# The memory rows as the moving operand: check and V projection turned round, and an If around the fallback loop

## The chip, the core and the metric

The kernel runs on one core of one Trainium2 chip. The time is device microseconds from start to end of one execution. Before the change the median of 6 runs is 1271.91 us (lowest 1271.03, highest 1274.84).

## The reference

Two independent parts are computed and their results are laid side by side in the last axis. Part A is a diagonal state-space layer (`h = Lam_bar * h + Bu` over 2048 steps, then a product with C). Part B is attention with a recurrent memory, and the change lies in it:

```python
for s in range(n_seg):                       # 64 segments of 32 rows
    h = jnp.concatenate([mem, xs], axis=1)   # 8 memory rows + 32 rows of x
    q, k, v = (jnp.einsum('btd,dhe->bhte', h, W) for W in (Wq, Wk, Wv))
    scores = jnp.einsum('bhqe,bhke->bhqk', q, k) * scale
    p = _softmax(jnp.where(mask, scores, -1e9), axis=-1)
    o = jnp.einsum('bhqk,bhke->bhqe', p, v)
    o = jnp.einsum('bhte,hed->btd', o, Wo)
    mem = o[:, :M, :].copy()                 # the next segment's memory
    outs.append(o[:, M:, :])
```

There are 32 heads of 128, the model width is 1024, and everything large is bf16. The memory of a segment is the output of the segment before, so the loop is serial as written.

## The kernel before

The kernel does not walk through the segments one after the other. It guesses the memory of every segment, computes all segments at once from the guess, and afterwards compares the memory that comes out with the guess. If they differ by more than a tolerance, a loop over the 64 segments (`general`, L795 on) computes part B again in the serial way; with the inputs given here the comparison holds and the loop runs no time.

Four stages follow each other, all bound to the same TensorE:

- **Stage 1** (0 to about 364 us): part A's scan, and V of all rows of x for the eight groups of four heads (`v_x`). V rows go to DRAM tensors `b_vx` and `b_vt`.
- **Stage 2** (to about 487 us): part A's product with C, 32 half tiles of 32 matmuls of 512 columns. Between them the guess is made (`guess`, L495): for each of eight chunks of 128 of the model width, 32 matmuls (one for each head) with a chunk of Wo as the stationary operand and 64 columns of `b_ogT` as the moving one, into one PSUM tile. Its result has the model width on partitions. DVE writes it to the memory columns of `b_xe` (`memT`, 73 columns: one for each memory row that is distinct) and once more to `b_gx`, in the order of the comparison. Eight PE transposes turn `b_gx` into rows, and DVE copies these to `b_gm` [73, 1024].
- **Attention** (to about 1047 us): Q and K projections (`proj`) and attention (`attention`) are generators whose steps are interleaved. A unit of attention is 4 score matmuls into `psS` (L607), Exp on ACT (L610), a mask product on POOL into one of five `b_m` tiles (L613), and for three blocks at a time a matmul with V into `psO` or `psR`, with a reciprocal and a product on DVE (L629, L630). The product of the masked scores is used by TensorE one to two units later.
- **Output projection** (to the end): 16 tiles of 128 rows in two halves, each 32 matmuls of 512 columns, evicted by DVE and ACT in turn and stored. After the tiles of block 1 `check` (L749) is run.

`v_mem` (L521) computes V of the 73 memory rows for one group of four heads: 8 matmuls with `memT` (128x73) stationary and 512 columns of `b_wv` moving, giving [73, 512] in a `psP` tile; DVE casts it into `b_vst` (L89), and SP issues two DMAs, to `b_vx` and `b_vt`. It is called twice in stage 2, and six times in the attention stage, every second head pair at the unit u = 4.

`check` takes `b_omT` (the attention outputs of the 73 memory rows, transposed) as the stationary operand and 512 columns of Wo as the moving one: 32 matmuls for each half. DVE subtracts `b_gm`, ACT squares the output and the difference, with a sum along each row (L767, L768). Some one-column operations of DVE make `c_bad` of it, a matmul with ones (`psR<-c_bad,ones`) gathers the partitions, and `b_flag` is 0 or 1. At the end every engine reads the flag into a register, multiplies it by 64 and enters the loop with that count (L1078).

`psP` has three buffers that rotate over all users; `psS` two, `psO` two, `psR` one. In stage 1 the order on PE and SP is that of the program. Later on, a scheduler puts the instructions of each engine in order and can move independent ones past each other. Every engine executes its own queue in that order. Nearly all matmuls and copies go through helpers, so their lines are L62 (PE and SP), L87 (ACT) and L89 (DVE), and the tiles' names tell them apart (`t` and `wo` are the two halves of Wo, `a_hl` and `t` in stage 2 are part A's operands).

Of the kernel before, what the change touches and what calls it, by code (L numbers as in the profile page):

```python
# [25 lines left out]
H = 32; E = 128; SEG = 32; M = 8; NSEG = 64; L = M + SEG  # L26
# [9 lines left out]
NM = NTL + NMX  # L36
# [296 lines left out]
class PartB:  # L333
    def __init__(self, k, x, mem0, Wq, Wk, Wv, Wo, out):
        self.k = k
        self.x, self.mem0, self.out = x, mem0, out
        self.Wf = [w.rearrange("(c p) h e -> p c (h e)", p=128) for w in (Wq, Wk, Wv)]
        self.Wo = Wo.rearrange("h e d -> e h d")
        self.vx = [k.drp.tile([NSLOT, 4 * EV], BF16, name=f"b_vx{i}") for i in range(HB)]
        self.vt = [k.drp.tile([NTL, 4 * EV], BF16, name=f"b_vt{i}") for i in range(HB)]  # L340
        self.on = [k.drp.tile([T, 1024], BF16, name=f"b_on{i}") for i in range(4)]
        self.tn = [k.drp.tile([NR, 1024], BF16, name=f"b_tn{i}") for i in range(4)]
        c = k.cst
        self.m0T = c.tile([128, KC, M], BF16, name="b_m0T")
        self.omT = c.tile([128, H, NR], BF16, name="b_omT")
        self.gm = c.tile([NM, D], BF16, name="b_gm")
# [148 lines left out]
    def guess(self, pool):  # L495
        k = self.k; V, PE = k.V, k.PE
        pg = k.ps("S")
        for q in range(4):
            wo = self.wog.pop(0)
            for dc in range(2):  # L500
                c = 2 * q + dc
                for h in range(H):
                    PE.matmul(pg[:, c * NSEG:(c + 1) * NSEG], wo[:, h, dc * 128:(dc + 1) * 128], self.ogT[:, h, :], start=(h == 0), stop=(h == H - 1))
                yield
        pv = pg[:].rearrange("p (c s) -> p c s", c=KC)
        m = self.memT
        V.tensor_copy(m[:, :, NMX + 1:NMX + 2], pv[:, :, 0:1])
        V.tensor_copy(m[:, :, NMX + 3:NM], pv[:, :, 1:NSEG])

        gx = pool.tile([128, KC, NM], BF16, name="b_gx", bufs=1)  # L510
        V.tensor_copy(gx[:, :, 0:2], pv[:, :, 0:2])
        V.tensor_copy(gx[:, :, 2:NTL - 1], pv[:, :, 1:NSEG])
        V.tensor_copy(gx[:, :, NTL - 1:NM], pv[:, :, 0:1].to_broadcast([128, KC, NMX + 1]))
        pt = k.ps("R", (128, 1024), BF16)
        for c in range(KC):
            PE.transpose(pt[0:NM, c * 128:(c + 1) * 128], gx[:, c, :], k.ident[:])
        V.tensor_copy(self.gm[:], pt[0:NM, :])
        yield


    def v_mem(self, hb, w=None):  # L521
        k = self.k
        w = w or self.load_wv(hb)
        p = k.ps("P")
        for c in range(KC):
            k.PE.matmul(p[0:NM, :], self.memT[:, c, :], w[:, c, :], start=(c == 0), stop=(c == KC - 1))
        st = self.next_st()
        k.copy("v", st[0:NM, 0, :, 0:E], p[0:NM, :].rearrange("p (h e) -> p h e", h=4))
        sv = st[:, 0, :, :].rearrange("p h e -> p (h e)")
        k.SP.dma_start(self.vx[hb][64:64 + NMX, :], sv[0:NMX, :])  # L530
        k.SP.dma_start(self.vt[hb][:], sv[NMX:NM, :])
# [217 lines left out]
    def check(self):  # L749
        k = self.k; V, S, PE = k.V, k.S, k.PE  # L750
        pool = self.p4

        def small(name, n):
            return pool.tile([128, n], FP32, name=name, bufs=1)
        for q in range(4):
            k.SP.dma_start_transpose(self.omT[:, 8 * q:8 * q + 8, :], self.tn[q][:])
        dn = small("c_dn", 4)
        V.memset(dn[:], 0.0)
        for half in range(2):
            hs = slice(half * 512, (half + 1) * 512)  # L760
            p = k.ps("P")
            for h in range(H):
                PE.matmul(p[0:NM, :], self.omT[:, h, 0:NM], self.wo[half][:, h, :], start=(h == 0), stop=(h == H - 1))
            df = pool.tile([NM, 512], FP32, name="c_df", bufs=1)
            jk = pool.tile([NM, 512], FP32, name="c_jk", bufs=1)
# [16 lines left out]
        V.tensor_scalar(bad[:], ok[:], -1.0, 1.0, ALU.mult, ALU.add)  # L782
        pf = k.ps("R")
        PE.matmul(pf[0:1, 0:3], k.ones[:], bad[:], start=True, stop=True)
        fl = small("c_fl", 1)
        V.tensor_reduce(fl[0:1, :], pf[0:1, 0:3], AX.X, ALU.max)
        V.tensor_scalar(fl[0:1, :], fl[0:1, :], 0.5, None, ALU.is_ge)
        V.tensor_copy(self.flag[:], fl[0:1, :])
        if getattr(k, "dbg", None) is not None:
            k.SP.dma_start(k.dbg[:, 0:4], dn[:])  # L790
            k.SP.dma_start(k.dbg[:, 4:7], ok[:])
        yield

# [117 lines left out]
def kernel_main(tc, A_x, A_Lre, A_Lim, A_Bre, A_Bim, A_Cre, A_Cim, A_logdt, A_Dskip, B_x, B_mem0, B_Wq, B_Wk, B_Wv, B_Wo, out,  # L911
                force=False, dbg=None):
    with ExitStack() as ctx:
        k = K(tc, ctx)
# [15 lines left out]
        with pool("p1x", "right") as p1x, pool("p1", "right", 1) as p1:  # L930
# [28 lines left out]
            for kind, pc, q in order[1:]:  # L959
# [9 lines left out]
                n = 4 * pc + q  # L969
# [173 lines left out]
```

## Time and profile before

| what | value |
|---|---|
| median of 6 runs | 1271.91 us (1271.03 to 1274.84) |
| the profiled execution | 1275.58 us |
| its span, first to last instruction | 1273.9 us |
| its mean granted TensorE clock | 0.994 |
| PE busy | 1252.8 us (98%), 7860 matmuls |
| DVE, POOL, ACT busy | 52%, 22%, 21% |
| last matmul, last ACT copy | about 1267.4 us; 1268.14 us |

A line of the timeline gives the start, the duration, engine, source line, operation, output and inputs, shapes and the number of instructions merged in it; a note in brackets is the idle time of the engine before it and what ended that. For matmuls, `128*73 128x512` is the stationary operand's size (partitions x columns) and then the moving operand's. Matmuls are pipelined: a row of several lasts until the last one has left the array, which is later than when the next row starts. The time that a matmul costs the stream is thus the distance between the starts of two rows, divided by the count, and not the mean duration.

### The profile page before, as it was taken

Reading aid. Unit: us, or ns where it says so; the run is one execution under the profiler, and the core shown is the slowest. Engines: PE = TensorE matmul, PEld = TensorE weight load, DVE = VectorE, ACT = ScalarE, POOL = GpSimd, SP = SyncE. Lnnn points to the kernel's source line nnn. Section 1 sums busy time; section 2 is a strip of 40 time slices with the busy share of each in tenths; the row PEclk is TensorE's granted clock in tenths of the full one; section 3 lists DMA queues with packets and bytes.
Section 4 is the critical chain, followed back from the end, with each engine's and each line's share of the span. In section 5 each row is a group of like instructions: output and inputs, shape, how many; then the busy total and the mean of one; then the engine's idle time right before and its main releaser. Section 6 shows DMA issues by size and latency. Waiting matters only on the chain. (4 is left out here: it accounts for less than half of the span.)

```text
span 1273.9 us, 19279 instructions
## 1 busy us (share of the span) xinstructions
PE 1252.8 (98%) x7860; PEld 655.8 (51%) x7860; DVE 665.7 (52%) x1235; ACT 263.3 (21%) x632; POOL 277.3 (22%) x407
## 2 busy tenths in 40 slices
PE   8899999999999999999999999999999999999997
PEld 4344444444445545565556555555655554444443
DVE  3687899998711123666666666656666641001000
ACT  4244334443310000121212111212211110001000
POOL 3111322222322220322322232223222220000000
PEclk9899999999999999999999999999999999999999
DMA  9965436544799629245464544636474389215000
GB/s 201 238 194 165 136 113 148 141 125 133 193 357 305 204 77 237 69 93 133 104 144 104 138 104 109 138 75 137 95 158 92 66 221 224 69 37 129 17 25 19
DMA packets 317156, 174.12 MB, mean 137 GB/s; under 512 B 140808, under 2 KB 302848, under 8 KB 317064
## 3 DMA queue, kind: packets, MB, share of 16 engines
q1 hardware_dynamic: 294504, 147.53, 48.3%
q10 hardware_dynamic: 21536, 22.16, 5.5%
q0 software_dynamic: 1024, 3.17, 0.8%
q8 instruction: 63, 1.03, 0.4%
q14 instruction: 29, 0.24, 0.1%
HBM read 86.42 MB, written 52.19 MB: 109 GB/s over the span
## 5 line engine op out<-in xcount | busy, mean ns | idle before, releaser
L62 PE MATMUL psP<-b_wv,b_xe 128*128 128x512 bf16 (+2 forms) x1112 | 243.1, 376 | 4.9 <-ACT b_vst L87 3.6
L62 PE MATMUL psP<-b_xe,b_wq 128*128 128x480 bf16 (+1 forms) x1280 | 247.8, 343 | 0.0
L62 PE MATMUL psP<-b_xe,b_wk 128*128 128x480 bf16 (+1 forms) x1280 | 247.7, 343 | 0.0
L613 POOL TENSOR_TENSOR b_m<-b_e,maskB 99x396 bf16<-99x396 bf16 x160 | 139.4, 871 | 338.8 <-ACT b_e L610 338.8
L610 ACT ACTIVATE b_e<-psS 99x396 bf16<-99x396 f32 x176 | 88.2, 501 | 545.1 <-PE psS L62 542.3
L62 PEld LDWEIGHTS <-b_xe 128*128 128x128 bf16 (+1 forms) x1112 | 109.6, 99 | 130.8 <-issue 6.0
L62 PEld LDWEIGHTS <-b_wk 128*128 128x128 bf16 x1280 | 119.7, 98 | 95.8
L62 PEld LDWEIGHTS <-b_wq 128*128 128x128 bf16 x1280 | 118.5, 98 | 88.2 <-issue 0.2
L89 DVE CAST b_k<-psP 128x480 bf16<-128x480 f32 (+1 forms) x192 | 98.0, 532 | 98.1 <-PE psP L62 98.1
L89 DVE CAST b_q<-psP 128x480 bf16<-128x480 f32 (+1 forms) x192 | 98.2, 533 | 93.4 <-PE psP L62 91.6
L62 PEld LDWEIGHTS <-b_ol 128*128 128x128 bf16 x832 | 81.3, 98 | 98.0
L62 PE MATMUL psU<-a_xT,a_bt 128*128 128x512 bf16 x512 | 117.7, 385 | 5.0 <-DMA a_xT<-in_A_x_dram 4.7
L62 PE MATMUL psP<-t,a_hl 128*128 128x512 bf16 x512 | 113.0, 379 | 0.0
L89 DVE CAST b_ost<-psP 128x512 bf16<-128x512 f32 x16 | 11.1, 692 | 185.2 <-PE psP L62 185.2
L87 ACT ACTIVATE b_vst<-psP 128x512 bf16<-128x512 f32 x126 | 72.5, 591 | 98.7 <-PE psP L62 89.5
L62 PE MATMUL psP<-wo,b_ol 128*128 128x512 bf16 x416 | 92.4, 379 | 0.0
L62 PE MATMUL psP<-t,b_ol 128*128 128x512 bf16 x416 | 92.2, 379 | 0.0
L276 POOL TENSOR_SCALAR a_tt<-a_pr,a_tabf 128x1 f32<-128x1 f32 x48 | 37.0, 771 | 250.2 <-DVE a_pr L271 250.2
L630 DVE TENSOR_TENSOR b_ob<-psO,b_accR 99x384 bf16<-99x384 f32 x160 | 86.0, 554 | 2.5
L263 DVE TENSOR_TENSOR a_pr<-psU,a_tabf 128x2048 f32<-128x2048 f32 x32 | 73.1, 2285 | 25.7 <-PE psU L62 25.7
L62 PEld LDWEIGHTS <-a_bt 128*128 128x128 bf16 x512 | 49.7, 99 | 65.1 <-issue 8.5
L62 PEld LDWEIGHTS <-a_hl 128*128 128x128 bf16 x512 | 49.2, 98 | 57.3
(186 smaller groups left out, 934.6 us busy)
## 6 DMA issues: line engine op xcount, KB each, us to landing
b_v<-b_vx SPq DMA_DIRECT2D x16, 1064.2 KB
b_wv<-in_B_Wv_dram SPq DMA_DIRECT2D x16, 1024.0 KB
b_on<-b_ob SPq DMA_DIRECT2D x15, 960.0 KB
b_vx<-b_vst ACTq DMA_DIRECT2D x24, 516.0 KB
a_hs<-a_h SPq DMA_DIRECT2D x32, 256.0 KB
b_wog<-in_B_Wo_dram SPq DMA_DIRECT2D x4, 2048.0 KB
b_wq<-in_B_Wq_dram SPq DMA_DIRECT2D x16, 512.0 KB
b_wk<-in_B_Wk_dram SPq DMA_DIRECT2D x16, 512.0 KB
```

The lines of the kernel that those rows point to most:

```text
L62: r = f(*a, **kw)
L87: self.S.activation(out, in_, ACT.Copy)
L89: self.V.tensor_copy(out, in_)
L263: V.tensor_tensor(pr[:], u[:].unsqueeze(1).to_broadcast([128, 2, 2, TB]), view(t3, [[TB + 1, 2], [TB + 1, 2], [1, TB]]), ALU.mult)
L276: G.tensor_scalar(tt[:, j:j + 1], w[:, j, TB - 1:TB], t3[:, 1, TB:TB + 1], None, ALU.mult)
L610: k.S.activation(e[:], s[0:GW], ACT.Exp, scale=float(E) ** -0.5, accum_out=self.accE[0:GW, i:i + 1])
L613: k.G.tensor_tensor(m[:, 0:4 * GW].rearrange("p (a b q) -> p a b q", a=2, b=2), e[:], mask[0:GW, :, :].unsqueeze(2).to_broadcast([GW, 2, 2 ...
L630: V.tensor_tensor(self.ob[:, b0:b0 + n, :], o[0:GW, 0:n, 0:E], r.unsqueeze(2).to_broadcast([GW, n, E]), ALU.mult)
```

## The change

The memory columns become the moving operand in both places, and the loop gets an If around it.

- `guess` keeps `b_gx` as it is (now a constant tile); its eight transposes and the copy to `b_gm` go.
- `v_mem` runs, for each of its four heads, 8 matmuls with 128x128 of `b_wv` stationary and the 73 columns of `memT` moving: 32 matmuls into four parts of one `psP` tile. DVE casts the tile to `b_vm` [128, 4, 73], four PE transposes bring it into a second `psP` tile, and DVE copies that to `b_vst`. The two DMAs stay.
- `check` runs, for each of the eight chunks of 128 of the model width, 32 matmuls with 128x128 of Wo stationary and 73 columns of `b_omT` moving: 256 matmuls. DVE subtracts `b_gx`, ACT squares both into `c_sq` without a sum, DVE reduces `c_sq` over the chunks to `c_ss` [128, 2, 73], two fp32 matmuls with a column of ones sum over the partitions into `psR`, and DVE copies that to `c_t2`. From there on it is as before.
- The loop is entered with the constant count 64 inside an If on the flag.

```diff
@@ guess
-        gx = pool.tile([128, KC, NM], BF16, name="b_gx", bufs=1)
+        gx = self.gx
         V.tensor_copy(gx[:, :, 0:2], pv[:, :, 0:2])
...
-        pt = k.ps("R", (128, 1024), BF16)
-        for c in range(KC):
-            PE.transpose(pt[0:NM, c * 128:(c + 1) * 128], gx[:, c, :], k.ident[:])
-        V.tensor_copy(self.gm[:], pt[0:NM, :])
@@ v_mem
-        for c in range(KC):
-            k.PE.matmul(p[0:NM, :], self.memT[:, c, :], w[:, c, :], start=(c == 0), stop=(c == KC - 1))
+        for h in range(4):
+            for c in range(KC):
+                k.PE.matmul(p[:, h * NM:(h + 1) * NM], w[:, c, h * 128:(h + 1) * 128], self.memT[:, c, :], start=(c == 0), stop=(c == KC - 1))
+        vm = self.vmp.tile([128, 4, NM], BF16, name="b_vm", bufs=1)
+        k.copy("v", vm[:], p[:, 0:4 * NM].rearrange("p (h n) -> p h n", h=4))
+        pt = k.ps("P", (128, 1024), BF16)
+        for h in range(4):
+            k.PE.transpose(pt[0:NM, h * 128:(h + 1) * 128], vm[:, h, :], k.ident[:])
         st = self.next_st()
-        k.copy("v", st[0:NM, 0, :, 0:E], p[0:NM, :].rearrange("p (h e) -> p h e", h=4))
+        k.copy("v", st[0:NM, 0, :, 0:E], pt[0:NM, 0:512].rearrange("p (h e) -> p h e", h=4))
@@ check
-        dn = small("c_dn", 4)
-        V.memset(dn[:], 0.0)
+        sq = pool.tile([128, 2, KC, NM], FP32, name="c_sq", bufs=1)
+        df = pool.tile([128, 4, NM], FP32, name="c_df", bufs=1)
         for half in range(2):
...
-            for h in range(H):
-                PE.matmul(p[0:NM, :], self.omT[:, h, 0:NM], self.wo[half][:, h, :], start=(h == 0), stop=(h == H - 1))
...
-            V.tensor_tensor(df[:], p[0:NM, :], self.gm[:, hs], ALU.subtract)
-            S.activation(jk[:], p[0:NM, :], ACT.Square, accum_out=dn[0:NM, 2 + half:3 + half])
-            S.activation(jk[:], df[:], ACT.Square, accum_out=dn[0:NM, half:half + 1])
+            for c in range(4):
+                for h in range(H):
+                    PE.matmul(p[:, c * NM:(c + 1) * NM], self.wo[half][:, h, c * 128:(c + 1) * 128], self.omT[:, h, 0:NM],
+                              start=(h == 0), stop=(h == H - 1))
+            pv = p[:, 0:4 * NM].rearrange("p (c n) -> p c n", c=4)
+            V.tensor_tensor(df[:], pv, self.gx[:, cs, :], ALU.subtract)
+            S.activation(sq[:, 1, cs, :], pv, ACT.Square)
+            S.activation(sq[:, 0, cs, :], df[:], ACT.Square)
+        ss = pool.tile([128, 2, NM], FP32, name="c_ss", bufs=1)
+        V.tensor_reduce(ss[:], sq[:].rearrange("p a c n -> p a n c"), AX.X, ALU.add)
+        onef = small("c_one", 1)
+        V.memset(onef[:], 1.0)
+        pd = k.ps("R")
+        for i in range(2):
+            PE.matmul(pd[0:NM, i:i + 1], ss[:, i, :], onef[:], start=True, stop=True)
+        t2 = small("c_t2", 2)
+        V.memset(t2[:], 0.0)
+        V.tensor_copy(t2[0:NM, :], pd[0:NM, 0:2])
         ok = small("c_ok", 3)
-        t2 = small("c_t2", 2)
-        V.tensor_tensor(t2[:, 0:1], dn[:, 0:1], dn[:, 1:2], ALU.add)
-        V.tensor_tensor(t2[:, 1:2], dn[:, 2:3], dn[:, 3:4], ALU.add)
@@ kernel_main
-        with tc.For_i(0, f0 * NSEG, 1) as it:
-            with tc.tile_pool(name="gen", bufs=1) as gp:
-                b.general(it, gp)
+        with tc.If(f0 == 1, preferred_fallthrough_block=False):
+            with tc.For_i(0, NSEG, 1) as it:
+                with tc.tile_pool(name="gen", bufs=1) as gp:
+                    b.general(it, gp)
```

In the order that the scheduler gives to the changed program, the four transposes of a stage-2 `v_mem` stand directly behind its 32 matmuls. In the attention stage a `v_mem`'s 32 matmuls are followed by the next unit's 4 score matmuls, 6 matmuls with V and one score matmul of the unit after that; then come the four transposes, and then the 16 K-projection matmuls that stood ahead of these before. In the check the two fp32 matmuls stand behind 13 of the next tile's matmuls, and `c_bad`'s matmul 5 further on. SP's, POOL's and ACT's orders are otherwise unchanged. At the end, each engine's way from the flag to the program's last block was a compare, a jump over the loop's body to the loop's exit block with 12 waits and a further jump on every engine, and the last block; it is now a compare and a jump straight to the last block, where SP alone has 12 waits.

More of the change, by code (lines that the diff above doesn't have):

```diff
@@ L345, in __init__ @@
         self.omT = c.tile([128, H, NR], BF16, name="b_omT")
-        self.gm = c.tile([NM, D], BF16, name="b_gm")
+        self.gx = c.tile([128, KC, NM], BF16, name="b_gx")
+        self.vmp = c
         self.xbar = c.tile([128, KC, NSEG], BF16, name="b_xbar")
@@ L756, in check @@
             k.SP.dma_start_transpose(self.omT[:, 8 * q:8 * q + 8, :], self.tn[q][:])
-        dn = small("c_dn", 4)
-        V.memset(dn[:], 0.0)
+        sq = pool.tile([128, 2, KC, NM], FP32, name="c_sq", bufs=1)
+        df = pool.tile([128, 4, NM], FP32, name="c_df", bufs=1)
         for half in range(2):
-            hs = slice(half * 512, (half + 1) * 512)
+            cs = slice(4 * half, 4 * half + 4)
             p = k.ps("P")
-            for h in range(H):
-                PE.matmul(p[0:NM, :], self.omT[:, h, 0:NM], self.wo[half][:, h, :], start=(h == 0), stop=(h == H - 1))
-            df = pool.tile([NM, 512], FP32, name="c_df", bufs=1)
-            jk = pool.tile([NM, 512], FP32, name="c_jk", bufs=1)
-            V.tensor_tensor(df[:], p[0:NM, :], self.gm[:, hs], ALU.subtract)
-            S.activation(jk[:], p[0:NM, :], ACT.Square, accum_out=dn[0:NM, 2 + half:3 + half])
-            S.activation(jk[:], df[:], ACT.Square, accum_out=dn[0:NM, half:half + 1])
-            yield
+            for c in range(4):
[6 more added lines that the diff above has]
+            S.activation(sq[:, 0, cs, :], df[:], ACT.Square)
+            yield
+        ss = pool.tile([128, 2, NM], FP32, name="c_ss", bufs=1)
[8 more added lines that the diff above has]
+        V.tensor_copy(t2[0:NM, :], pd[0:NM, 0:2])
         ok = small("c_ok", 3)
-        t2 = small("c_t2", 2)
-        V.tensor_tensor(t2[:, 0:1], dn[:, 0:1], dn[:, 1:2], ALU.add)
-        V.tensor_tensor(t2[:, 1:2], dn[:, 2:3], dn[:, 3:4], ALU.add)
         V.tensor_scalar(t2[:, 1:2], t2[:, 1:2], TOL * TOL, None, ALU.mult)
@@ L789, in check @@
         if getattr(k, "dbg", None) is not None:
-            k.SP.dma_start(k.dbg[:, 0:4], dn[:])
+            k.SP.dma_start(k.dbg[:, 0:2], t2[:])
             k.SP.dma_start(k.dbg[:, 4:7], ok[:])
```

## The prediction

> **What bounds the kernel now.** I read the page's engine shares first, then what PE waited for, then the timeline at the places that the change touches.
>
> ```profile
> PE 1252.8 (98%) x7860; PEld 655.8 (51%) x7860; DVE 665.7 (52%) x1235; ACT 263.3 (21%) x632; POOL 277.3 (22%) x407
> ```
>
> Next the list of PE's waits, whole span, the two longest and the longest outside the first stage (total, times, longest):
>
> ```profile
> PE psU L62 <- DMA a_xT<-in_A_x_dram: 4.7, 1, 4.7
> PE psP L62 <- ACT b_vst L87: 3.6, 2, 3.0
> ...
> PE psO L62 <- POOL b_m L613: 0.8, 3, 0.4
> ```
>
> TensorE is the bound everywhere. Nearly all its waiting is in the first stage; in stage 2, the attention and the output projection it has next to none. So what the change takes from or adds to PE's stream there moves the end by as much, and DVE, ACT and POOL count only where PE comes to wait for them.
>
> What a matmul costs PE's stream is the distance between starts. The timeline of PE in the last guess step and at the transposes that go:
>
> ```profile
> 448.42 1.10 PE L62 MATMUL psS<-b_ogT,b_wog 128*128 128x64 bf16 x32
> 449.35 7.07 PE L62 MATMUL psP<-t,a_hl 128*128 128x512 bf16 x32
> 456.26 0.61 PE L62 MATMUL psR<-ident,b_gx 128*73 128x128 bf16 x8
> 456.71 3.62 PE L62 MATMUL psP<-t,a_hl 128*128 128x512 bf16 x16
> ```
>
> 32 matmuls of 64 columns, each with its own 128x128 weights, take 0.93 us: 29.1 ns each. 32 of 512 columns take 6.91 us: 215.8 ns. 8 transposes of 128 columns take 0.45 us: 56 ns. The score matmuls below, 99 columns, take 0.18 us for four: 44.5 ns. Between 64 and 99 columns, 73 columns come to 29.1 + 9/35 x 15.4 = **33.0 ns**, an interpolation. The guess is just the form of the new matmuls: its weight loads are hidden.
>
> **The change, part by part.** All sums are against the profiled execution (1275.58 us; span 1273.9). It is 3.67 us above the median, and I carry the difference over to the median.
>
> *1. The guess's transposes* (8, and DVE's 73x1024 copy of 0.68 us, off the path): **-0.45 us**.
>
> *2. v_mem in stage 2, twice.* The first of them before:
>
> ```profile
> 470.52 1.89 PE L62 MATMUL psP<-b_wv,b_xe 128*73 128x512 bf16 x8
> 472.25 7.07 PE L62 MATMUL psP<-t,a_hl 128*128 128x512 bf16 x32
> ```
>
> 8 x 216 ns = 1.73 us, and PE goes on at once. After, 32 x 33.0 = 1.06 us, then the transposes stand directly behind and have to wait: the last matmul drains (0.20 from its start, as a 64-column one has 0.193, so 0.17 past its slot), DVE starts 0.1 later, casts 128x292 in about 0.46 (128x256 took 0.419 and 128x480 0.659), PE takes it up in 0.06 to 0.25, and the four transposes cost 0.23. Sum 2.1 to 2.3 against 1.73: +0.35 to +0.55 each, **+0.9** for both. The rows queued behind on PE are part A's matmuls; DVE's own queue is free there (part A's one subtraction, 0.69 us, is over before the drain), and the two DMAs on SP issue some 0.9 us later, 26 us before the first use of `b_v`.
>
> *3. v_mem in the attention, six times.* The first, all engines:
>
> ```profile
> 581.08 0.34 PE L62 MATMUL psS<-b_q,b_k 128*128 128x99 bf16 x4
> 581.26 0.34 PE L62 MATMUL psO<-b_v,b_m 99*128 99x129 bf16 x3
> 581.44 1.89 PE L62 MATMUL psP<-b_wv,b_xe 128*73 128x512 bf16 x8
> ...
> 582.19 0.87 POOL L613 TENSOR_TENSOR b_m<-b_e,maskB 99x396 bf16<-99x396 bf16 x1 [2.73 <-ACT b_e L610]
> ```
>
> 1.73 us becomes 1.06 + 0.23 = 1.29. But the order also pulls the next unit's matmuls in front of the 16 of K's projection, which were the cover of the mask chain. From the scores' start (581.08) to the end of POOL's product is 1.98 us (583.06), and PE takes it 0.06 later (that is the step at 1030.42 to 1030.48), so 2.04. In the new order PE reaches the two matmuls that need that mask after 0.36 + 1.06 + 0.18 + 0.18 + 0.06 = 1.84: a stall of 0.2. The `b_vm` cast, for which DVE is free after its product for `b_ob`, at 582.62 = 1.54, starts near 1.7, ends near 2.2, as PE arrives: no further stall. Each: -1.73 + 1.29 + 0.2 = -0.24, **-1.45** for six. Bounds: -0.45 each if the stall is none (-2.7), and 0 if the transposes wait 0.25 more. SP's DMAs to `b_vx` and `b_vt` go out 0.9 us later, and behind them in SP's queue the next `b_wq` load; `b_v` is loaded 27 us later and those weights used a head pair (34 us) later, so neither is seen.
>
> *4. The check.* PE before:
>
> ```profile
> 1142.40 7.07 PE L62 MATMUL psP<-t,b_omT 128*73 128x512 bf16 x32
> 1149.31 7.07 PE L62 MATMUL psP<-wo,b_omT 128*73 128x512 bf16 x32
> 1156.22 2.97 PE L62 MATMUL psP<-t,b_ol 128*128 128x512 bf16 x13
> 1159.48 0.17 PE L62 MATMUL psR<-c_bad,ones 128*1 128x3 bf16 x1 [0.29 <-DVE c_bad L782]
> 1159.58 4.27 PE L62 MATMUL psP<-t,b_ol 128*128 128x512 bf16 x19
> ```
>
> 1142.40 to 1156.22 is 13.82 us for 64 matmuls; 256 x 33.0 = 8.45: -5.37. Behind it the chain to the fp32 matmuls: DVE starts 0.2 after the last slot (1149.31 to 1149.51), subtracts 292 columns in 0.46, ACT squares twice (0.41, 0.43 by its 256- and 396-column rows), DVE reduces 1168 elements in about 1.36 (704 took 0.877, 176 took 0.329): 3.0 us with the handovers, while PE gets there after 13 x 0.216 = 2.8: 0.2 of stall. The two fp32 matmuls are in no row; between 0.05 (two of the cheapest pitch here) and 0.8 (eight weight load rows of 98 ns, as far as I would go), I take 0.2, since one column is streamed. Then `c_bad` waits for five small DVE steps (five x 0.19, with handovers 1.3) against 5 x 0.216 = 1.08: 0.3 with its matmul, where before the gap from 1159.02 to 1159.58 was 0.56. Part: **-5.2**, between -5.6 and -4.3.
>
> The trace is against a rule here. The Trainium skill, "TensorE: Matmul & The Clock Gate", section "Back-to-back issue gap", gives about 81 ns for a weight load and matmul pair of 128 columns in a real kernel's stream, and would make the 256 about 20.7 us by that estimate, dearer than the 13.8 they replace. This trace has 29.1 ns at 64 columns and 56 ns at 128, and the measurement decides.
>
> *5. The If.* PE's last matmul starts its slot at 1267.1; ACT's copy ends at 1268.14, SP issues the last store at 1268.16, its packets end by 1271.0, and the span ends at 1273.9. Between these two, in the window of the last two microseconds, the instruction queues move:
>
> ```profile
> q8 instruction: 1, 0.02, 3.4%
> q14 instruction: 1, 0.01, 1.7%
> ```
>
> q8 carries PE's code (63 packets over the span for 15720 matmuls and weight loads, 250 each). Its packet here moves at 1272.0, after the store has landed. In the new program PE, DVE, ACT and POOL can jump to the last block without waiting for the store. SP's own waits (12 before, 12 after) stay. What can go is one jump and a fetch, at most from 1271.0 to 1272.2; what can come is a fetch that now falls on SP (the 0.5 us from 1272.0 to the other packet at 1272.55). I take **-0.5**, between -1.2 and +0.5.
>
> The Trainium skill, "Runtime: NRT & Kernel Launch", section "Instruction fetch mechanics", says a jump out of the prefetched pages makes the engine wait for a fetch; it gives no price, and the two packets agree with it.
>
> **Sum:** -0.45 + 0.9 - 1.45 - 5.2 - 0.5 = **-6.7 us**: 1268.9 for the profiled execution, **1265.2** for the median. The lower ends add to -0.45 + 0.7 - 2.7 - 5.6 - 1.2 = -9.25 (1262.7), the upper to -0.45 + 1.1 + 0 - 4.3 + 0.5 = -3.15 (1268.8).
>
> **Rivals.** *A, slower: weight loads become the bound.* A weight load row lasts 98 ns and the guess has only 32 in a run; if a run of 128 with new weights is not hidden as 32 are, the pitch goes from 33 towards 98. 512 new pairs: 46 ns each uses up the 6.7, 51 ns makes it slower by 0.2%, 98 ns gives 1265.2 + 512 x 65 ns = 1298. Against it: 29.1 ns held in each of eight guess steps with no drift. *B, same: the new round trip stalls the attention.* `v_mem` now needs two of the three `psP` tiles and a DVE cast in mid-stream; if PE loses 0.9 us more at each of the six, 5.4 of the 6.7 go: 1270.6. For it: POOL's chain has 0.2 us too little already, and the three POOL waits of before (from 1030 us on) come where no projection gives cover. Against: DVE is idle half the time. *C, same: code supply in the check.* 512 PE instructions in 8.5 us are two packets of q8 in that time, where the output projection has one per 27 us. If each costs 2 us of stall, with the tail no better, 1265.2 + 4 + 0.5 = 1269.7. Against: in the guess steps packets come 12.7 us apart and PE waits for none.
>
> **Chances.** Forecast 0.80, A 0.06, B 0.08, C 0.06. 0.2% is 2.5 us, about what a measurement of this kernel can tell: same is 1269.4 to 1274.5. The forecast's bounds lie below that, B and C inside it, A's likeliest prices above. Faster 0.80, same 0.14, slower 0.06. The range goes from the lower ends' sum past the upper ends' sum and C to B: 1262.7 to 1270.6.
>
> **What would show it.** PE in the check: eight runs of 32 of 73 columns, 1.06 us from start to start; if above 1.5, A. A gap of 0.2 to 0.4 before `psR<-c_one,c_ss`. The two stage-2 `v_mem`: a gap of 0.8 to 1.0 before the transposes; in the attention six new waits of psR for POOL near 0.2; if they are near 1, B. The q8 packet after the store gone, and under 2.9 us from the store's landing to the end. The prediction is wrong above all if 73 columns don't go at 33 ns.

## The result and the profile after

The changed kernel takes **1267.43 us** (median of 19 runs, 1264.75 to 1271.8), against 1271.84 for the kernel before beside it (44 runs). The ratio is 0.9967, with a 95% interval of 0.9959 to 0.9976: 4.2 us less, between 3.05 and 5.2. The forecast was 6.7 us less, 1265.2 in a range from 1262.7 to 1270.6. A second set of runs of the same kernel, given among the experiments, has 5.6 us less (0.9956, 0.9942 to 0.997). So the direction is right, the time lies in the range, and the gain is smaller than predicted, by about a third in the first set. Two executions of other kernels below took far longer than the rest (3408.13 us with `v_mem` alone, 6349.21 us without the If and shifted); their medians and ratios are given without them, and no run shows what happened there.

The profiled execution took 1268.61 us, its span is 1266.9 (before: 1275.58 and 1273.9), at a granted clock of 0.996 (0.994). Cut at the same instructions of PE and ACT in both traces, the two spans are these:

| stretch, us | before | after | difference | predicted |
|---|---|---|---|---|
| stage 1, to the first matmul with `a_hl` | 363.11 | 361.25 | -1.86 | 0 |
| stage 2, to the first 201-column Q projection | 124.68 | 124.87 | +0.19 | -0.45 + 0.9 |
| attention, to the first matmul with `b_ol` | 559.65 | 558.21 | -1.44 | -1.45 |
| output projection, to the first matmul with `b_omT` | 94.96 | 94.96 | 0 | 0 |
| check and the rest of its tile | 21.29 | 17.12 | -4.17 | -5.2 |
| rest, to the end of ACT's last copy | 104.45 | 104.45 | 0 | 0 |
| tail, from there to the end of the span | 5.76 | 6.04 | +0.28 | -0.5 |

Stage 1 contains nothing of the change, and its length differs from profile to profile: from 357.5 to 363.3 us over the fourteen profiles of this study, largely with the clock that TensorE was granted. From 33 to 42 us the mean granted clock is 0.62 in the profile before, 0.81 after, and 1.00 in the two profiles with the shortest stage 1; from 354 to 363 us it is 0.81 before and after, and 1.00 in those two. PE's wait for its input `a_xT` differs too: 4.7 us before, 3.9 after. Whole executions show the same: of 35 of the kernel before on one chip, those with a mean clock of 0.999 took 1269.84 to 1270.65 us, those with 0.995 took 1273.88 to 1275.57. Without stage 1 the difference is -5.14 us, which is what the trace gives for the change; the measured interval of the times reaches to -5.2.

The engine line of the page after:

```profile
PE 1244.7 (98%) x8272; PEld 660.0 (52%) x8272; DVE 668.1 (53%) x1243; ACT 262.1 (21%) x628; POOL 277.4 (22%) x407
```

PE has 412 more matmuls than before and is busy for 8.1 us less. It is still the bound. The list of PE's waits after, whole span (total, times, longest):

```profile
PE psU L62 <- DMA a_xT<-in_A_x_dram: 3.9, 1, 3.9
PE psP L62 <- ACT b_vst L87: 3.4, 2, 2.8
...
PE psP L62 <- DVE b_vm L89: 1.1, 2, 0.6
PE psR L62 <- DVE c_ss L775: 0.9, 1, 0.9
...
PE psO L62 <- POOL b_m L616: 0.8, 3, 0.4
```

Two of these are new: the two `v_mem` of stage 2 wait for the cast of `b_vm`, and the check waits for the reduction `c_ss`. The timeline of PE after, first at a `v_mem` of stage 2, then at the check (start, length, what, and in brackets the idle time before):

```profile
468.21 1.24 PE L62 MATMUL psP<-b_xe,b_wv 128*128 128x73 bf16 x32
470.01 0.42 PE L62 MATMUL psP<-ident,b_vm 128*73 128x128 bf16 x4 [0.56 <-DVE b_vm L89]
470.26 7.07 PE L62 MATMUL psP<-t,a_hl 128*128 128x512 bf16 x32
...
1139.29 4.49 PE L62 MATMUL psP<-b_omT,t 128*128 128x73 bf16 x128
1143.62 4.49 PE L62 MATMUL psP<-b_omT,wo 128*128 128x73 bf16 x128
1147.94 2.97 PE L62 MATMUL psP<-t,b_ol 128*128 128x512 bf16 x13
1151.86 0.40 PE L62 MATMUL psR<-c_one,c_ss 128*73 128x1 f32 x4 [0.94 <-DVE c_ss L775]
1152.11 1.24 PE L62 MATMUL psP<-t,b_ol 128*128 128x512 bf16 x5
1153.28 0.17 PE L62 MATMUL psR<-c_bad,ones 128*1 128x3 bf16 x1
```

From start to start, a `v_mem` of stage 2 is now 470.26 - 468.21 = 2.05 us (1.73 before). In the check, 256 matmuls take 1147.94 - 1139.29 = 8.65 us, 33.8 ns each, in place of 13.82 us. Then PE runs out of the 13 matmuls that cover the chain and stands for 0.94 us. All engines after, without the rows of the weight loads (PEld), at the first `v_mem` of the attention and at the end of the check's chain:

```profile
579.72 1.24 PE L62 MATMUL psP<-b_xe,b_wv 128*128 128x73 bf16 x32
...
580.47 0.87 POOL L616 TENSOR_TENSOR b_m<-b_e,maskB 99x396 bf16<-99x396 bf16 x1 [2.72 <-ACT b_e L613]
580.80 0.34 PE L62 MATMUL psS<-b_q,b_k 128*128 128x99 bf16 x4
580.98 0.34 PE L62 MATMUL psO<-b_v,b_m 99*128 99x129 bf16 x3
581.00 0.46 DVE L89 CAST b_vm<-psP 128x292 bf16<-128x292 f32 x1
581.16 0.53 PE L62 MATMUL psR<-b_v,b_m 99*128 99x129 bf16 x3
...
581.58 0.38 PE L62 MATMUL psP<-ident,b_vm 128*73 128x128 bf16 x4
...
1148.70 0.42 ACT L771 ACTIVATE c_sq<-psP 128x292 f32<-128x292 f32 x1 [3.64 <-DVE c_df L770]
1149.01 0.44 ACT L772 ACTIVATE c_sq<-c_df 128x292 f32<-128x292 f32 x1
1149.48 2.23 DVE L775 TENSOR_REDUCE c_ss<-c_sq 128x146 f32<-128x1168 f32 x1 [0.82 <-ACT c_sq L772]
```

POOL's product ends at 581.34, in the middle of the row with `psR`, which lasts 0.53 us, where the same form lasts 0.34 elsewhere: that is the predicted stall of 0.2, and the transposes behind it wait for nothing. The weight loads in front of that row wait 0.19 to 0.20 us for POOL's product at each of the six calls, and at none of these places before. In the check the reduction takes 2.23 us.

### The profile page after: what moved, and what is told of

Read it like the earlier page. It is cut to its first block, busy times and chain, and to the rows that moved or that the text cites. A ratio compares the mean times of both kernels' runs of the same rounds, so it can differ in the third digit from the quotient of the medians.

```text
span 1266.9 us, 20042 instructions
## 1 busy us (share of the span) xinstructions
PE 1244.7 (98%) x8272; PEld 660.0 (52%) x8272; DVE 668.1 (53%) x1243; ACT 262.1 (21%) x628; POOL 277.4 (22%) x407
## 5 line engine op out<-in xcount | busy, mean ns | idle before, releaser
L62 PE MATMUL psP<-b_wv,b_xe 128*128 128x512 bf16 (+1 forms) x1048 | 228.1, 376 | 4.1 <-ACT b_vst L87 3.4
L62 PEld LDWEIGHTS <-b_xe 128*128 128x128 bf16 x1048 | 102.7, 98 | 124.8 <-issue 5.8
```

Source lines behind the costliest of these rows:

```text
L62: r = f(*a, **kw)
```

## The experiments

Each kernel was timed beside the kernel before on the same chip. Ratios are to that, with 95% intervals, and are not quite the quotients of the two medians; where "one execution" stands, only a single one was made, and its profile is read.

**The If alone.** The kernel before, with its loop over a count from a register put into an If.

```diff
-        with tc.For_i(0, f0 * NSEG, 1) as it:
-            with tc.tile_pool(name="gen", bufs=1) as gp:
+        with tc.If(f0 == 1, preferred_fallthrough_block=False):
+            with tc.For_i(0, NSEG, 1) as it:
...
```

> The kernel before with the If around the fallback loop alone. In the two profiles the time from the last copy on ACT to the end of the span went from 5.76 to 6.04 us. Theory (TensorE's stream carries the gain, the If gives nothing): that stretch is 5.7 to 6.1 us, the ratio to before 0.9996 to 1.0006. Rival 1 (the If costs, and is why the medians show 4.2 us where the two profiles' parts sum to 5.1): 6.5 us or more, ratio 1.0005 to 1.0010. Rival 2 (the jump straight to the last block saves what the prediction had): 5.3 us, ratio 0.9996 or less.

Measured: 1271.97 against 1272.37 us, ratio 1.0003 (0.9992 to 1.0015). The tail is 5.83 us against 5.76. So in the program before, the If is worth nothing.

**Guess and check alone.** The changed kernel, with `v_mem` and the loop as before.

```diff
-        for h in range(4):
-            for c in range(KC):
-                k.PE.matmul(p[:, h * NM:(h + 1) * NM], w[:, c, h * 128:(h + 1) * 128], self.memT[:, c, :], start=(c == 0), stop=(c == KC - 1))
...
+        for c in range(KC):
+            k.PE.matmul(p[0:NM, :], self.memT[:, c, :], w[:, c, :], start=(c == 0), stop=(c == KC - 1))
...
-        with tc.If(f0 == 1, preferred_fallthrough_block=False):
...
+        with tc.For_i(0, f0 * NSEG, 1) as it:
...
```

> The guess's transposes gone and the check turned round; V of the memory rows and the loop's entry as before. Theory: the guess gives 0.45 us, the check 4.2 (stretch from its first matmul to the start of the matmuls of the tile behind next 17.1 us, where before has 21.3), so -4.6 us, ratio 0.9964. Rival (the check's shorter stream is given back later, at the stores or the last wait): the stretch is 17.1 us too, but the ratio is 0.998 or above.

Measured: 1269.54 us, ratio 0.9977 (0.9966 to 0.9988). Stage 2 is 124.23 us, 0.45 less than before, which is the guess's transposes exactly; the check is 17.38 us, 3.91 less; the tail is 5.65. So most of the whole gain is here, though the expected 0.9964 lies just below the interval. Nothing is given back at the stores or at the end, as the rival had it: the rest behind the check is 104.45 us, as before. Two things in its profile were not expected. The attention is 560.43 us, 0.78 more than before, with one wait of PE for DVE's `b_q` of 0.67 us near 496 us. DVE is late there because it first stood 4.03 us for a store of part A (`out_dram<-a_ot`), before it cleared part of `b_q`. It stands there in every kernel, in twelve of the fourteen profiles for 2.55 to 3.48 us; the one other profile with a longer stand (4.09) has the same wait of PE (0.74). So the lengthening comes of a transfer that landed late in these two, and not of the check; why it landed late is open. And the second half of the check takes 4.59 us where the first takes 4.33, with one gap of 0.21 us in the weight loads that no engine released; the long run below says what that is like.

**The turned `v_mem` alone.** The kernel before with the new `v_mem`, its cast kept in a part of the staging tile that is not used.

```diff
-        for c in range(KC):
-            k.PE.matmul(p[0:NM, :], self.memT[:, c, :], w[:, c, :], start=(c == 0), stop=(c == KC - 1))
+        for h in range(4):
+            for c in range(KC):
+                k.PE.matmul(p[:, h * NM:(h + 1) * NM], w[:, c, h * 128:(h + 1) * 128], self.memT[:, c, :], start=(c == 0), stop=(c == KC - 1))
...
+        vm = st[:, 1, :, 0:NM]
+        k.copy("v", vm, p[:, 0:4 * NM].rearrange("p (h n) -> p h n", h=4))
+        pt = k.ps("P", (128, 1024), BF16)
+        for h in range(4):
+            k.PE.transpose(pt[0:NM, h * 128:(h + 1) * 128], vm[:, h, :], k.ident[:])
...
```

> V of the memory rows turned round alone; the cast copy stands in an unused part of b_vst, since the extra tile does not fit beside b_gm. Theory: the two calls in stage 2 cost 0.32 us each (2.05 us from their first matmul to part A's next, against 1.73), the six in the attention give 0.24 each, so -0.8 us, ratio 0.9994. Rival (the order of the attention behind each call is worse by more than the trace of one call shows): the attention stage, from its first projection matmul to the first matmul of b_ol, is longer than 558.6 us, and the ratio is above 1.0.

Measured: 1272.54 us over eleven executions, against 1272.37, ratio 1.0008 (0.9997 to 1.0018), so the expected small gain (0.9994) is missed: it lies just below the interval. The profile does show both expected signs: stage 2 +0.93 us, attention -1.45 us (558.20, below the rival's 558.6). The sum, half a microsecond, is less than the times can settle, but they speak for no gain at all rather than for this one.

**Guess, check and `v_mem`, without the If.** The changed kernel with the loop as before (the reverse of the first diff).

> The changed kernel with the loop entered as before (count from the flag, no If). Theory: same stream as the changed kernel, last copy on ACT to the end 5.7 to 6.1 us, ratio to before 0.9958 to 0.9968. Rival 1 (the If costs about 1 us): last copy to the end shorter by 0.5 us or more than in the changed kernel, ratio 0.9958 or less.

Measured: 1269.84 against 1272.37 us, ratio 0.9984 (0.9973 to 0.9996), less gain than with the If, which neither the theory nor its rival had. Stage 2 (125.07), attention (558.20) and check (17.12) are those of the changed kernel to 0.2 us. What differs is the tail, 8.45 us, where 5.7 to 6.1 was expected. The timeline of SP near the end of this kernel, with the span above it:

```profile
core 0 of [0], span 1268.1 us
...
1259.67 0.33 SPq L62 DMA_DIRECT2D out_dram<-b_ost  x1
```

The last store is issued 8.4 us before the span ends, where it is 6.0 us in the changed kernel. By the tails, then, the If is worth 2.4 us here, and in the program before nothing: what it is worth depends on the program around it. In this tail the queue of PE's code moves three packets, 8.2, 4.6 and 0.4 us before the end; before and after the change it moves two.

**The same with the code shifted.** To test whether it is the place of the code, 16 one-column matmuls were put into the warm-up of the kernel without the If. The row of these matmuls lasts 4.47 us with them and 4.45 without; they move everything behind them by 32 PE instructions.

```diff
+        for _ in range(16):
+            k.PE.matmul(p[:, 0:1], w[:, 0:128], w[:, 0:1], start=True, stop=True)
```

> e4 (the changed kernel without the If) with 16 matmuls of one column in the same place: the exit block stands 213 to 225 instructions into a block of 256. Theory: the last copy to the end is 5.6 to 6.1 us again, the stages as in the changed kernel, ratio 0.9955 to 0.9975. Rival (the If itself shortens the end of the new code): 8.2 to 8.7 us as in e4, ratio 0.998.

Measured: 1266.95 us over five executions, against 1272.44, ratio 0.9958 (0.9945 to 0.9971). The tail is 5.52 us, 2.93 shorter than without the shift, and two packets of PE's code move in it. The interval lies wholly below that of the unshifted kernel (0.9973 to 0.9996). So the shift alone gives back all that the If gave.

**The kernel before, shifted the wrong way.** 26 such matmuls in the kernel before, which bring the loop's exit block to where it lay in the kernel without the If.

```diff
+        for _ in range(26):
+            k.PE.matmul(p[:, 0:1], w[:, 0:128], w[:, 0:1], start=True, stop=True)
```

> The kernel before with 26 matmuls of one column behind the ten warming ones, where PE waits for its first input: 52 PE instructions more in front, so that the loop's exit block stands 182 to 194 instructions into a block of 256, as in e4 (181 to 193), where before has 130. Theory (the 2.4 us that e4's end is longer are one more fetch of PE's code, since the exit block and the last block fall across two blocks): last copy to the end 8.2 to 8.7 us, the stages as before, ratio 1.0010 to 1.0030. Rival (the long end of e4 comes of its longer program, or is chance): 5.6 to 6.1 us, ratio 0.9995 to 1.0008.

Measured: a tail of 7.53 us, against 5.76 unshifted. Two packets of PE's code move in it and a third just after the span's end. That is nearer to the theory (8.2 to 8.7) than to its rival (5.6 to 6.1), but in neither range. The time does not follow: 1272.24 against 1272.44 us, ratio 1.0001 (0.999 to 1.0012), where 1.0010 to 1.0030 was expected. In this profile stage 1 is 357.61 us, at the short end, but so it is in the profile of `v_mem` alone, which has no added matmuls (357.48), and in both the clock stays at 1.00 there. So the longer tail is seen in one profile and the other executions do not show its cost; whether their tails are shorter is open.

**No fallback at all** (one execution). The changed kernel without the read of the flag and without the fallback loop, which this kernel leaves out of the program.

```diff
-        f0 = nc.values_load(b.flag[0:1, 0:1], min_val=0, max_val=1)
-        with tc.If(f0 == 1, preferred_fallthrough_block=False):
-            with tc.For_i(0, NSEG, 1) as it:
-                with tc.tile_pool(name="gen", bufs=1) as gp:
-                    b.general(it, gp)
```

> The changed kernel without the fallback loop and without reading the flag: the guess is compared, but nothing is done if it fails. Theory (the end's length comes of PE's code fetched after a jump): no jump is left, one fetch at most in sequence, the store's landing to the end 2.9 us or less, last copy to the end 5.0 to 5.6 us. Rival (the barrier and the semaphore resets at the end set it): 5.6 to 6.1 us, as with the loop.

Measured: 1264.97 us. SP's timeline near the end:

```profile
core 0 of [0], span 1263.3 us
...
1260.06 0.33 SPq L62 DMA_DIRECT2D out_dram<-b_ost  x1
```

The tail is 3.27 us, well below the theory's 5.0 to 5.6 and its rival's 5.6 to 6.1, and no packet of PE's code moves after the store. So by the tails a loop that is never entered costs this program between 2.2 and 5.2 us at its end, depending on the kernel. The tails together (us; the packets' and the landing's times are before the end of the span, read in steps of 0.2 us and rounded up; the place is the exit or last block's position in PE's code modulo 256 instructions, counted in the compiled program):

| kernel | tail | last store landed | PE code packets | place |
|---|---|---|---|---|
| no fallback | 3.27 | 1.6 | none | - |
| no If, shifted | 5.52 | 3.2 | 5.2, 2.0 | 213-225 |
| `v_mem` alone (no If) | 5.62 | 3.0 | 5.2, 1.8 | 66-78 |
| guess and check alone (no If) | 5.65 | 3.0 | 5.2, 1.8 | 245-1 |
| before (no If) | 5.76 | 3.0 | 5.0, 1.8 | 130-142 |
| If alone | 5.83 | 3.6 | 5.6, 2.4 | 145-148 |
| after (If) | 6.04 | 3.8 | 5.8, 2.0 | 196-199 |
| before, shifted (no If) | 7.53 | 4.8 | 7.2, 3.6 | 182-194 |
| no If, not shifted | 8.45 | 5.8 | 8.2, 4.6, 0.4 | 181-193 |

The changed kernel, profiled a second time, had a tail of 6.45 us, so differences of 0.4 us in this column say nothing. Part of the cost is in the store itself: from ACT's copy to the landing it takes 1.7 us without the fallback and 2.2 to 2.8 with it; the rest comes after the landing.

**The reduction's layout** (one execution). The changed kernel with the squares laid out so that the reduction reads neighbours and ACT writes with a step of 8, instead of the other way round.

```diff
-        sq = pool.tile([128, 2, KC, NM], FP32, name="c_sq", bufs=1)
+        sq = pool.tile([128, 2, NM, KC], FP32, name="c_sq", bufs=1)
...
-            S.activation(sq[:, 1, cs, :], pv, ACT.Square)
-            S.activation(sq[:, 0, cs, :], df[:], ACT.Square)
+            S.activation(sq[:, 1, :, cs].rearrange("p n c -> p c n"), pv, ACT.Square)
+            S.activation(sq[:, 0, :, cs].rearrange("p n c -> p c n"), df[:], ACT.Square)
...
-        V.tensor_reduce(ss[:], sq[:].rearrange("p a c n -> p a n c"), AX.X, ALU.add)
+        V.tensor_reduce(ss[:], sq[:], AX.X, ALU.add)
```

> The changed kernel with c_sq laid out so that DVE's reduction reads neighbouring elements (ACT writes with a step of 8 instead). Theory (the reduction took 2.23 us and not 1.36 because it reads with a step of 73 elements): the reduction takes 1.3 to 1.5 us, PE's wait for c_ss falls from 0.94 to below 0.3 us. Rival (the many short sums cost it, not the step): 2.2 us still.

Measured: 1270.91 us in this one execution, with a stage 1 of 363.30. Its timeline at the end of the check's chain:

```profile
1150.80 0.70 ACT L771 ACTIVATE c_sq<-psP 128x292 f32<-128x292 f32 x1 [3.13 <-DVE c_df L770]
1151.29 0.74 ACT L772 ACTIVATE c_sq<-c_df 128x292 f32<-128x292 f32 x1
1152.06 1.37 DVE L775 TENSOR_REDUCE c_ss<-c_sq 128x146 f32<-128x1168 f32 x1 [1.29 <-ACT c_sq L772]
...
1153.58 0.39 PE L62 MATMUL psR<-c_one,c_ss 128*73 128x1 f32 x4 [0.56 <-DVE c_ss L775]
```

The reduction takes 1.37 us in place of 2.23, but each square 0.70 to 0.74 in place of 0.42 to 0.44, so that PE's wait falls only from 0.94 to 0.56 (below 0.3 was expected) and the check from 17.12 to 16.73. The step in the layout is paid on one side or the other.

**The parts that gain, put together.** The changed kernel, with the old `v_mem` in stage 2 and the check's last part one tile block later, so that the reduction has a whole tile to hide in.

```diff
+        if w is not None:
+            return self.v_mem_rows(hb, w)
...
-                    for _ in b.check():
+                    chk = b.check()
+                    next(chk)
+                    next(chk)
+                if tb == 2:
+                    for _ in chk:
```

> The changed kernel with the two stage-2 calls of v_mem in the old form (weights moving, no round trip), and with the check's reduction, its two fp32 matmuls and the flag's chain one block of tiles later. Theory: 0.6 us back in stage 2, 1.0 us in the check (its stretch of matmuls 8.65 us, and no wait for c_ss behind it); last copy to the end 5.7 to 6.1 us. So 1.7 us less than the changed kernel: ratio to before 0.9945 to 0.9965. Rival (PE's stalls there are covered elsewhere): same as the changed kernel, 0.9967.

Measured: 1267.38 against 1272.44 us, ratio 0.9965 (0.9953 to 0.9978). The timeline of PE in the check, whose end is now a tile later:

```profile
1138.32 4.49 PE L62 MATMUL psP<-b_omT,t 128*128 128x73 bf16 x128
1142.64 4.75 PE L62 MATMUL psP<-b_omT,wo 128*128 128x73 bf16 x128
1147.23 7.07 PE L62 MATMUL psP<-t,b_ol 128*128 128x512 bf16 x31
...
1202.48 0.36 PE L62 MATMUL psR<-c_one,c_ss 128*73 128x1 f32 x4
1202.70 1.24 PE L62 MATMUL psP<-t,b_ol 128*128 128x512 bf16 x5
1203.88 0.17 PE L62 MATMUL psR<-c_bad,ones 128*1 128x3 bf16 x1
```

There is no wait for `c_ss` any more, stage 2 is 0.64 us shorter than in the changed kernel, and check and rest together 0.88 us. The times cannot tell the two kernels apart.

**The same without the If, and the changed kernel once more beside it.** The first is the kernel above with the loop as before; the second is the changed kernel with no edit.

> e7 without the If: old v_mem in stage 2, the check's last part one block of tiles later, the loop entered as before; its exit block stands 70 instructions into a block of 256. Theory: the stages as in e7 (stage 2 124.2 us), last copy to the end 5.5 to 5.8 us against 6.3 in e7, ratio to before 0.9948 to 0.9962, and 0.7 to 2 us below the changed kernel run beside it. Rival (what the trace shows gained in stage 2 and the check is lost elsewhere): as the changed kernel, 0.9967.

> The changed kernel itself, on the same chip as e7 without the If. Theory: -0.45 + 0.64 - 1.44 - 4.17 + 0.28 = -5.1 us by the stages of the two profiles, ratio 0.9955 to 0.9970.

Measured on one chip: 1267.45 us, ratio 0.9956 (0.994 to 0.9972), and 1267.94 us, ratio 0.9956 (0.9942 to 0.997). In the first one's profile the tail is 5.66 us against 6.45, stage 2 is 124.46 against 125.18, and check and rest are 120.43 against 121.57, but the attention is 0.87 longer, with the wait for `b_q` (0.74 us) that the second experiment had. The expected 0.7 to 2 us between the two is not in the times. So no version here that keeps the fallback was measured to be faster than the changed kernel.

**A long run of short matmuls** (one execution). The changed kernel with 512 further matmuls of the check's form ahead of the check, 256 of 73 columns and 256 of 32, whose results are not used.

```diff
+        junk = pool.tile([128, 1], FP32, name="c_junk", bufs=1)
+        for n in (NM, 32):
+            px = k.ps("P")
+            for c in range(4):
+                for h in range(H):
+                    PE.matmul(px[:, c * n:(c + 1) * n], self.wo[0][:, h, c * 128:(c + 1) * 128], self.omT[:, h, 0:n], start=(h == 0), stop=(h == H - 1))
+            for c in range(4):
+                for h in range(H):
+                    PE.matmul(px[:, c * n:(c + 1) * n], self.wo[1][:, h, c * 128:(c + 1) * 128], self.omT[:, h, 0:n], start=(h == 0), stop=(h == H - 1))
+            V.tensor_copy(junk[:, 0:1], px[:, 0:1])
```

> The changed kernel with 512 more matmuls in front of the check's 256, each with its own 128x128 weights of Wo: 256 of 73 columns and 256 of 32, so 768 in one run, 1536 PE instructions. Theory (weight loads and code supply stay hidden): 8.65 us for each 256 of 73 columns, 6.4 to 7.0 for those of 32 (the 4-column matmuls of stage 1 stand 25 ns apart), some 24 us in all, the time after it shifted by 15.0 to 15.7. Rival A (weight loads bind in a long run) or C (code supply binds): the third 256 takes over 11 us, or the 32-column ones are no faster than the 73-column ones, and gaps without a releaser of 1 us or more show in the run.

Measured: the 768 matmuls take from 1139.14 to 1166.61, 27.47 us, where 24 were expected. The timeline of PE in this kernel:

```profile
1139.14 4.49 PE L62 MATMUL psP<-b_omT,t 128*128 128x73 bf16 x128
1143.46 4.49 PE L62 MATMUL psP<-b_omT,wo 128*128 128x73 bf16 x128
1147.79 3.39 PE L62 MATMUL psP<-b_omT,t 128*128 128x32 bf16 x128
1151.03 0.20 PE L62 MATMUL psP<-b_omT,wo 128*128 128x32 bf16 x2
1152.40 3.33 PE L62 MATMUL psP<-b_omT,wo 128*128 128x32 bf16 x126 [1.17 <-issue]
1155.58 0.23 PE L62 MATMUL psP<-b_omT,t 128*128 128x73 bf16 x2
1157.50 4.42 PE L62 MATMUL psP<-b_omT,t 128*128 128x73 bf16 x126 [1.69 <-issue]
1161.75 0.23 PE L62 MATMUL psP<-b_omT,wo 128*128 128x73 bf16 x2
1162.36 4.42 PE L62 MATMUL psP<-b_omT,wo 128*128 128x73 bf16 x126 [0.37 <-issue]
```

The first 386 matmuls go without a gap, those of 73 columns at 33.8 ns and those of 32 at 25.3 ns (1147.79 to 1151.03 for 128). Then PE stands three times, for 1.17, 1.69 and 0.37 us, each time 128 matmuls, that is 256 PE instructions with their weight loads, after the time before, and no engine releases it. The restarts are 5.10 and 4.86 us apart, whatever the number of columns. The queue of PE's code moves one packet in each of the microseconds from 1144, 1150, 1154, 1159, 1163 and 1166; in the changed kernel's check these are 1144, 1155 and 1171. So the supply of code is the limit of a long run, at about 5 us per 256 instructions, and the check's 256 matmuls end before it binds.

## Why the prediction was right, and where its sizes were off

**Step 1, the guess's transposes** (-0.45): as predicted. The kernel with guess and check alone has just 0.45 us less in stage 2.

**Step 2, `v_mem` in stage 2** (+0.9): the cost is there, at the place and by the wait that was predicted, but smaller: +0.32 each, +0.64 in all. PE's gap is 0.56 us, or 0.72 counted from the last matmul's slot, where the prediction had 0.8 to 1.0; DVE starts 0.04 us after the drain where 0.1 was assumed, and PE takes up 0.06 us after the cast, the low end of what was allowed. The kernel with `v_mem` alone has +0.93, with its waits at 0.62.

**Step 3, `v_mem` in the attention** (-1.45): -1.44 in the changed kernel and -1.45 with `v_mem` alone. The stall of 0.2 us on POOL's mask product is in the row of `psR` (0.53 for 0.34) and in the weight loads ahead of it at all six calls, and DVE's cast meets no queue. The condition of rival B, 0.9 us more at each, did not come.

**Step 4, the check** (-5.2, between -5.6 and -4.3): -4.17, just outside its bounds. The pitch of the 256 matmuls (the distance between their starts) was right, 33.8 ns for 33.0, which is 0.2 us. The term that was mis-sized is the reduction. The prediction took 1.36 us from rows with 704 and 176 elements; it takes 2.23, because it reads with a step of 73 elements. The layout experiment, where it reads neighbours, has 1.37, so the count was right and the step was not thought of. PE stood 0.94 us; counted as the prediction did, from the last of the 13 slots, it lost 1.1 in place of 0.2. The fp32 matmuls cost 0.25 us for the 0.2 taken, and `c_bad` about 0.2 for 0.3. This is most of what the forecast missed.

On the rule weighed there: the Trainium skill, "TensorE: Matmul & The Clock Gate", section "Back-to-back issue gap", gives 81 ns for a pair of weight load and matmul at 128 columns in a kernel's stream. The runs here do not agree: the trace before has 56 ns at 128 columns, and the runs after have 33.8 ns at 73 and 25.3 at 32, each with its own weights. The formula that the section keeps for a single matmul, N / 2.4 + 2.5 ns with a floor of about 25, gives 32.9 ns and 25 for these, as an estimate, and fits them.

**Step 5, the If** (-0.5, between -1.2 and +0.5): +0.28 in the profile, within its bounds, and no gain. Its sign is not sure, since the same kernel's tail was 6.45 us in its second profile, 0.4 more; both profiles speak against the -0.5. The prediction expected the packet of PE's code behind the store to vanish and less than 2.9 us from landing to end; the packet is still there, 2.0 us before the end, and from landing to end it is 3.8. So taking the other engines' 12 waits away did not bring the end forward; which engine's fetch ends last is not to be read from the packets. What the step missed is that this stretch depends on where the code lies: the same If is worth nothing in the program before and 2.4 us in the changed one, and 32 PE instructions more in front are worth as much. This rests on the tails and the times of the changed kernel without the If; in the shifted kernel before, the tail alone shows it.

**The sum.** In the profiles -0.45 + 0.64 - 1.44 - 4.17 + 0.28 = -5.14, against -6.7: 1.0 of the difference is the check, 0.8 the If, and 0.3 goes the other way in stage 2. The times of the first set give -4.2, between -3.05 and -5.2, and the second set -5.6, between -3.8 and -7.4. Means over executions of the same granted clock (0.996, 0.997, 0.998 and 0.999; 56 of the kernel before from three chips, 17 of the changed one) differ by 4.2 to 4.8 us. Together they point to some 4 to 5.5 us; only the second set's interval reaches the forecast's 6.7. The experiments' single ratios (1.0003, 0.9977, 1.0008) multiply to 0.9988 where the whole is 0.9967. That is about as far apart as their intervals allow; how often the late transfer of 0.7 us in the profile of guess and check alone came in its other executions is not known.

**The rivals.** A, weight loads as the bound, is refuted: 128 loads in a row are hidden as 32 are. B is refuted by step 3. C, the supply of code, has a real mechanism but did not bind here: no gap in the check of the changed kernel, one of 0.2 us in two other kernels (guess and check alone, and the parts that gain put together), and gaps of up to 1.7 us only from the 387th short matmul on. The guess steps could not have shown it: there the packets came 12.7 to 19.2 us apart, and not at 12.7 throughout.

## What to carry to other kernels

When few columns meet large weights, make the few columns the moving operand: the pitch falls with the columns as long as the weight loads stay hidden, and a row of the same form elsewhere in the trace gives the price. Then look at what the turned result does to the work behind it, above all to the layout that a reduction has to read, and put work of PE behind each new round trip to another engine. A fallback that is never entered is not free at the program's end; before a branch is praised or blamed for a microsecond or two, shift the code by a few instructions and measure again. And compare executions of the same granted clock before a difference of a few microseconds is believed.

## What the runs showed of the hardware that was not expected

- In the profiles, the end of the program, from ACT's last copy on, took 3.27 us without the fallback, 5.5 to 6.6 with it, and 7.5 to 8.45 where the loop's exit block lay at 181 to 194 modulo 256 in PE's code. The Trainium skill, "Runtime: NRT & Kernel Launch", section "Instruction fetch mechanics", says that code comes in blocks of 256 instructions and that a jump to a block that has not been fetched waits for it. The packets in the tails agree; why this place and not the others is not settled by these runs, and for the kernel before the times did not follow the longer tail.
- The same section holds that fetching in sequence is hidden. The long run does not agree: 256 PE instructions per about 5 us were all that came, so that by this run short matmuls come to some 39 ns each in the long term (5 us / 128), as an estimate.
- A sum over 8 elements in fp32 with a step of 73 elements took 2.23 us for 1168 elements and 1.37 without a step; ACT's writes of 292 elements with a step of 8 took 0.70 to 0.74 us and 0.42 to 0.44 without.
- Stage 1 took 357.5 to 363.3 us in fourteen profiles with nothing of the change in it, a spread larger than the whole effect that was measured. It goes with the granted clock: 0.62 from 33 to 42 us in one of the longest (363.11), 1.00 there in the two shortest. Single executions of this kernel tell little; cutting the span at the same instructions tells much.
